# Unread identity products in TensorE's first waits, a first tile normalized in halves, and a later weight decode

## The chip, the cores and the metric

The kernel runs on one core of a Trainium2 chip. The metric is the device time of one execution in microseconds (us); lower is better. TensorE (PE) multiplies, VectorE (DVE) and ScalarE (ACT) work elementwise, GpSimd (POOL) does small things beside them, and SyncE (SP) issues most DMAs. Each engine takes its instructions in the order in which they stand in its queue.

## The reference

Three layers follow each other, for 8 batches of 576 rows and a model width of 512 (8 heads of 64). Cut to what matters:

```
kv  = einsum('bhsd,bhse->bhde', k, v)
out = einsum('bhsd,bhde->bhse', q, kv)
x   = out / sqrt(mean(out*out, -1) + 1e-6) * g_norm       # attention, a norm per head

theta  = x @ w_theta                                      # first mixing layer
zr, zi = x * cos(theta), x * sin(theta)
y = einsum('ts,bsd->btd', w_tok_r, zr) + einsum('ts,bsd->btd', w_tok_i, zi)
u = x + y;  x = u + relu(u @ w_ch)

h = relu(x.T @ w_tok1) @ w_tok2                           # second mixing layer
u = x + h.T;  out = u + relu(u @ w_ch1) @ w_ch2
```

## The kernel before

The weights arrive as 64-bit floats. ACT and DVE decode them into float32: `decode` is one ACT operation and three DVE operations a tile. Nearly every product is then made of three float16 products of high and low parts (`mm3`, L105 to L107). Batch 0 alone is different at its start: its first products run in float32, since nothing is split yet.

That start is what the change touches. A list of words in the main body (L1027) says in which order units of work are recorded for batch 0, and a scheduler orders each engine's queue from that record. The units are generators; every `yield` puts the rest of a unit one step later in the record, and `tc.keep_in_program_order` pins an instruction to its place in it. The units are, in the order of the data:

- `theta_weight(j)`: loads and decodes tile j (of 4) of `w_theta` into `wt` (tiles `wt0r` to `wt3r` hold the raw words).
- `kv`: 40 products of 64x64 from `k` and `v` into one PSUM bank `kvp`, in five groups of 8, one for each pair of loads; ACT and DVE copy the result into `kvbd`.
- `attend(o, r)` (a0 to a4; tile 4 holds the last 64 rows): four products `po`; a square on ACT (L471), a sum on DVE (`ss`, L473), an addition and a power on POOL (`ri`, L474 and L475), the multiplication that makes `x` on DVE (L478), and for batch 0 four transposes on PE (`px`, L488) that ACT copies into `xt` (L490).
- `rotate(o, r)` (r0 to r4): `pt` = xt times `wt` (L563, and L604 for tile 4), then sine and cosine on ACT (`cs`), products with `x` (L586), and the split into `zh` and `zl`.
- `mix_weights`: five tiles `wm0v`, `wm1v`, `wm8v`, `wm2v`, `wm3v` of the token weights, decoded (L164 on ACT; L172, L173, L174 on DVE) and split into `wmh` (ACT, L245) and `wml` (DVE, L247), in between the units above.
- `outer(o, r)` (X0 to X4): the mixing products `pa` and `pb`, float16, which need `zh`, `zl`, `wmh`, `wml`.

DMA engines load all of this in the first 43 us in the order in which SP issues it.

Of the kernel before, what the change touches and what calls it, by code (L numbers as in the profile page):

```python
# [10 lines left out]
F16 = mybir.dt.float16  # L11
F32 = mybir.dt.float32
I32 = mybir.dt.int32
AF = mybir.ActivationFunctionType
ALU = mybir.AluOpType
AX = mybir.AxisListType
# [3 lines left out]
P = 128  # L20
# [8 lines left out]
def attn_mixer_kernel(  # L29
# [4 lines left out]
    nc = tc.nc  # L34
    B, S, DM = k.shape
    D = g_norm.shape[0]
    H = DM // D
# [26 lines left out]
    def bank(name):  # L64
        return ps.tile([P, 512], F32, tag="ps", name=name)
# [48 lines left out]
    nc.gpsimd.memset(rows, 0.0)  # L114
    nc.scalar.dma_start(rows[:1].rearrange("p (i d) -> p i d", d=D), g_norm.unsqueeze(0).unsqueeze(1).to_broadcast([1, P // D, D]))
    pg = bank("pg")
    nc.tensor.transpose(pg[:, :P], rows, ident)
    nc.vector.tensor_copy(gn, pg[:, :1])
    gt, gs = (const.tile([P, 1], F32, name=name) for name in ("gt", "gs"))
# [38 lines left out]
            mybir.DependencyInfo(mybir.DependencyClass.NoSync, mybir.DependencyReason.DATA), reason="behind",  # L158
        )

    def decode(val, raw, behind=None):

        bits = val.bitcast(I32)
        first = nc.scalar.activation(val, raw[..., 1].bitcast(F32), AF.Copy, scale=2.0**-112)  # L164
        if behind is not None:
            gated(first, behind)
        if wp:

            tc.keep_in_program_order(first)
        yield  # L170
        place = placed if wp else lambda ins: ins
        place(nc.vector.tensor_scalar(bits, bits, 3, None, ALU.logical_shift_left))  # L172
        place(nc.vector.scalar_tensor_tensor(bits, raw[..., 0], 29, bits, ALU.logical_shift_right, ALU.bitwise_or))  # L173
        place(nc.vector.scalar_tensor_tensor(bits, raw[..., 1], -(2**31), bits, ALU.bitwise_and, ALU.bitwise_or))  # L174
# [23 lines left out]
    def theta_weight(j):  # L198

        if w_theta.dtype == F32:  # L200
            load(wt[:, j], w_theta[j * P:(j + 1) * P])
            yield
        else:
            raw = stg.tile([P, S, 2], I32, tag="raw", name=f"wt{j}r")[:, :DM]
            load(raw.rearrange("p n w -> p (n w)"), w_theta.bitcast(I32)[j * P:(j + 1) * P])
            yield
            yield from decode(wt[:, j], raw)

    def theta_split(j):

# [214 lines left out]
    def held(o, ins):  # L425
        if o.b == 0:
            tc.keep_in_program_order(ins)

    def kv(o, part):

        if part == 0:
            o.kp = bank(f"kvp{o.b}")[:, :HP * D].rearrange("p (h e) -> p h e", h=HP)
        for r in KV[part]:
            kt, vt = o.kv[2 * r:2 * r + 2]
            for hp in range(HP):
                for i in range(2):
                    cs = slice((2 * hp + i) * D, (2 * hp + i + 1) * D)
                    nc.tensor.matmul(
                        o.kp[i * D:(i + 1) * D, hp, :], kt[:, cs], vt[:, cs],
                        start=r == 0 and hp == 0, stop=r == NR and hp == HP - 1,  # L440
                    )
        if part:
            nc.scalar.activation(kvbd[:D, :, :D], o.kp[:D], AF.Copy)
            nc.vector.tensor_copy(kvbd[D:, :, D:], o.kp[D:])
        yield
        for r in KV[part]:
            if len(o.kv) < 2 * (NR + 1):
                load_kv(o, r + 3)

    def attend(o, r):  # L450
# [17 lines left out]
        x3 = x.rearrange("p (h d) -> p h d", d=D)  # L468
        place = beside(o)
        yield  # L470
        place(nc.scalar.activation(x3, po3, AF.Square, scale=D**-0.5))  # L471
        yield
        held(o, place(nc.vector.tensor_reduce(ss, x3, axis=AX.X, op=ALU.add)))  # L473
        nc.gpsimd.tensor_tensor(ss, ss, eps, ALU.add)  # L474
        nc.gpsimd.tensor_tensor(ri, ss, mhalf, ALU.pow)  # L475
        yield
        yield
        held(o, place(nc.vector.tensor_tensor(x3, po3, ri.unsqueeze(2).to_broadcast([P, H, D]), ALU.mult)))  # L478
        n = SR if r == NR else P
        R, by = o.R[:, :, r * P:r * P + n], SW if r == NR else gs  # L480
        if r == NR and b == 2:
# [52 lines left out]
    def prepare(o):  # L534
        if o.zh is None:

            o.zh = zp.tile([P, KM + 1, DM], F16, tag="zh", name=f"zh{o.b}")
            o.zl = zp.tile([P, KM - 1, DM], F16, tag="zl", name=f"zl{o.b}")
# [446 lines left out]
    def go(unit, lead=False):  # L985
        advance()
        next(unit)
        (leading if lead else pending).append(unit)
# [10 lines left out]
    def flush():  # L999
        while pending or leading:  # L1000
            advance()
# [17 lines left out]
            load_q(o, P)  # L1019
    for part in range(2):  # L1020
        go(kv(o, part))
    prepare(o)
    nc.gpsimd.memset(o.zh[:, 0, :1], 0.0)
    extra += mix_weights()
    nxt = load_heads(1)
    later = channel_weights()
    for what in "a0 . . a1 a4 a2 a3 r0 w r1 r4 w r2 r3 X0 X1 k w w w X4 A0 X2 A1 s0 s1 s2 s3 X3 A4 A2 A3 U".split():  # L1027
        if what == ".":
            advance()
        elif what == "w":  # L1030
            spare()
        elif what == "k":
            for part in range(2):
                go(kv(nxt, part))
        elif what == "U":
            go(mixed(o))
        else:
            unit = {"a": attend, "r": rotate, "X": outer, "s": residual}[what[0].replace("A", "a")]
            go(unit(nxt if what[0] == "A" else o, int(what[1])))
    flush()  # L1040
    extra += later

# [164 lines left out]
```

## Time and profile before

| | |
|---|---|
| median of 3 runs | 1086.23 us (1085.38 to 1087.14) |
| profiled execution, device time | 1085.04 us |
| its span, first to last instruction | 1083.3 us |
| busy, share of the span: PE | 1065.4 us, 98% |
| DVE | 806.9 us, 74% |
| ACT | 565.0 us, 52% |
| POOL | 188.7 us, 17% |

PE is busy nearly all the time, so a change of the time is a change of when PE gets its work at the start, or of what it waits for later. The timeline of one engine shows each instruction's start, its duration, and in brackets how long the engine sat idle before it and what ended that. The chain of waits and the list of PE's waits give the same from PE's side.

### The profile page before, as it was taken

Reading aid. Unit: us, or ns where it says so; the run is one execution under the profiler, and the core shown is the slowest. Engines: PE = TensorE matmul, PEld = TensorE weight load, DVE = VectorE, ACT = ScalarE, POOL = GpSimd, SP = SyncE. Lnnn points to the kernel's source line nnn. Section 1 sums busy time; section 2 is a strip of 40 time slices with the busy share of each in tenths; the row PEclk is TensorE's granted clock in tenths of the full one; section 3 lists DMA queues with packets and bytes.
Section 4 is the critical chain, followed back from the end, with each engine's and each line's share of the span. In section 5 each row is a group of like instructions: output and inputs, shape, how many; then the busy total and the mean of one; then the engine's idle time right before and its main releaser. Section 6 shows DMA issues by size and latency. Waiting matters only on the chain.

```text
span 1083.3 us, 21466 instructions
## 1 busy us (share of the span) xinstructions
PE 1065.4 (98%) x8857; PEld 813.4 (75%) x8857; DVE 806.9 (74%) x1431; ACT 565.0 (52%) x950; POOL 188.7 (17%) x256
## 2 busy tenths in 40 slices
PE   6999999999999999999999999999999999999998
PEld 5677776777668777686777777777777777777776
DVE  4999888788968888788463866858585775858484
ACT  3868456375554655647241736454463645446360
POOL 3140042624517335252000000000000000000000
PEclk9999999999999999999999999999999999999999
DMA  9618369748669387543738111020201101020101
GB/s 361 244 30 243 77 153 264 194 120 221 172 160 242 98 234 188 134 143 74 222 109 288 54 39 51 16 73 12 78 1 46 44 28 61 12 77 8 38 2 44
DMA packets 141366, 126.05 MB, mean 116 GB/s; under 512 B 88212, under 2 KB 117524, under 8 KB 141268
## 3 DMA queue, kind: packets, MB, share of 16 engines
q1 hardware_dynamic: 135888, 104.23, 34.7%
q0 software_dynamic: 5376, 20.45, 5.3%
q8 instruction: 69, 1.13, 0.4%
q14 instruction: 29, 0.24, 0.1%
q10 hardware_dynamic: 4, 0.00, 0.0%
HBM read 74.25 MB, written 29.88 MB: 96 GB/s over the span
## 4 chain that ended last, share of the span: by engine, by line
PE 77%; DVE 9%; DMA 5%; ACT 5%; POOL 2%; issue 1%; SPq 0%; DVEq 0%; POOLq 0%; ACTq 0%
PE pa L105 5%; PE pa L107 5%; PE pa L106 5%; PE na L105 4%; PE na L107 4%; PE na L106 4%; PE py L105 3%; PE py L107 3%; PE py L106 3%; DMA xt<-xs 3%; PE pr L105 2%; PE pr L107 2%; PE pr L106 2%; PE pc L107 2%; PE pc L106 2%; PE pc L105 2%
## 5 line engine op out<-in xcount | busy, mean ns | idle before, releaser
L105 PE MATMUL py<-wmh,zh 128*128 128x320 f16 (+1 forms) x468 | 134.2, 287 | 0.2 <-DMA zh<-zt 0.2
L106 PE MATMUL py<-wml,zh 128*128 128x320 f16 (+1 forms) x468 | 134.2, 287 | 0.0
L107 PE MATMUL py<-wmh,zl 128*128 128x320 f16 (+1 forms) x416 | 119.3, 287 | 0.0
L107 PE MATMUL na<-gh,wbl 128*128 128x288 f16 x384 | 109.3, 286 | 0.0
L106 PE MATMUL pa<-o,wah 128*128 128x288 f16 x384 | 109.2, 286 | 0.0
L106 PE MATMUL na<-gl,wbh 128*128 128x288 f16 x384 | 109.1, 286 | 0.0
L105 PE MATMUL pa<-o,wah 128*128 128x288 f16 x384 | 108.4, 286 | 0.0
L107 PE MATMUL pa<-o,wal 128*128 128x288 f16 x384 | 107.8, 286 | 0.0
L105 PE MATMUL na<-gh,wbh 128*128 128x288 f16 x384 | 106.0, 286 | 0.2
L870 DVE TENSOR_TENSOR gl<-sum,gh 128x1152 f16<-128x1152 f32 x48 | 65.0, 1354 | 21.9 <-ACT gh L869 21.9
L106 PEld LDWEIGHTS <-wbh 128*128 128x128 f16 x672 | 65.7, 98 | 17.8 <-issue 1.0
L106 PEld LDWEIGHTS <-wah 128*128 128x128 f16 x672 | 65.8, 98 | 16.6
L105 PEld LDWEIGHTS <-wah 128*128 128x128 f16 x672 | 65.8, 98 | 16.6
L105 PEld LDWEIGHTS <-wbh 128*128 128x128 f16 x672 | 65.7, 98 | 16.6
L107 PEld LDWEIGHTS <-wal 128*128 128x128 f16 x672 | 65.7, 98 | 16.6
L107 PEld LDWEIGHTS <-wbl 128*128 128x128 f16 x672 | 65.7, 98 | 16.6
L106 PE MATMUL pr<-ul,wch 128*128 128x256 f16 (+1 forms) x256 | 73.0, 286 | 0.0
L105 PE MATMUL pr<-uh,wch 128*128 128x256 f16 (+1 forms) x256 | 72.9, 286 | 0.0
L107 PE MATMUL pr<-uh,wcl 128*128 128x256 f16 (+1 forms) x256 | 72.8, 286 | 0.0
L475 POOL TENSOR_TENSOR ri<-ss,mhalf 128x8 f32<-128x8 f32 x40 | 69.8, 1744 | 2.5
L105 PEld LDWEIGHTS <-zh 128*128 128x128 f16 x576 | 56.4, 98 | 17.0 <-ACT zh L590 1.1
L869 ACT ACTIVATE gh<-sum 128x1152 f16<-128x1152 f32 x48 | 55.6, 1158 | 25.6 <-DVE sum L917 25.6
(304 smaller groups left out, 2922.0 us busy)
## 6 DMA issues: line engine op xcount, KB each, us to landing
c<-u2d SPq DMA_DIRECT2D x32, 288.0 KB, 4.5
out<-c SPq DMA_DIRECT2D x64, 144.0 KB, 1.7
q<-in_q SPq DMA_DIRECT2D x6, 1280.0 KB, 6.9
k<-in_k SPq DMA_DIRECT2D x26, 256.0 KB, 5.6
v<-in_v SPq DMA_DIRECT2D x26, 256.0 KB, 5.5
wa_r<-in_w_ch SPq DMA_DIRECT2D x24, 256.0 KB, 4.3
wb_r<-in_w_ch SPq DMA_DIRECT2D x24, 256.0 KB, 3.8
wad<-wa POOLq DMA_DIRECT2D x24, 224.0 KB, 3.7
```

The costliest lines, as they stand in the source:

```text
L105: nc.tensor.matmul(acc, ah, bh, start=first and i == 0, stop=False, **more)
L106: nc.tensor.matmul(acc, ah, bl, start=False, stop=False, **more)
L107: nc.tensor.matmul(acc, al, bh, start=False, stop=last and i == n - 1, **more)
L475: nc.gpsimd.tensor_tensor(ri, ss, mhalf, ALU.pow)
L869: nc.scalar.activation(h.hi[:, 3:], h.s, AF.Copy)
L870: nc.vector.tensor_tensor(h.lo[:, 3:], h.s, h.hi[:, 3:], ALU.subtract)
```

## The change

Four edits, all in what batch 0 records first. `keep_going(n)` records n products of a float16 view of the identity matrix, 256 columns each, into a PSUM bank `unread` that nothing reads: 18 ahead of everything, 2 ahead of each `kv` group but the first, 6 behind the last group, 8 behind `po` of tile 0 (40 in all). The `kv` products are pinned to their place in the record. Tile 0 alone is squared, summed, raised to the power and multiplied in two halves of four heads (`heads`). Tiles 2 and 3 of `w_theta` have their three DVE operations recorded 5 and 6 steps later and pinned. The list of words moves r0 ahead of a2.

```diff
@@ main body @@
+    unread = bank("unread")
+    eye16 = ident.bitcast(F16)
+
+    def keep_going(n):
+
+        for _ in range(n):
+            tc.keep_in_program_order(nc.tensor.matmul(unread[:, :2 * P], eye16[:, :P], eye16, start=True, stop=True))
+
+    keep_going(18)
     nc.tensor.transpose(pg[:, :P], rows, ident)
@@ decode @@
         yield
-        place = placed if wp else lambda ins: ins
+        for _ in range(ticks):
+            yield
+        place = placed if wp else tc.keep_in_program_order if ticks else lambda ins: ins
@@ theta_weight @@
-            yield from decode(wt[:, j], raw)
+            yield from decode(wt[:, j], raw, ticks=6 if j == KD - 1 else 5 if j == 2 else 0)
@@ kv @@
+            if o.b == 0 and r:
+                keep_going(2)
...
-                    nc.tensor.matmul(
+                    held(o, nc.tensor.matmul(
@@ attend @@
+        heads = [slice(0, H)] if b or r not in (0,) else [slice(0, H // 2), slice(H // 2, H)]
+        for h in heads:
+            place(nc.scalar.activation(x3[:, h], po3[:, h], AF.Square, scale=D**-0.5))
+        yield
+        for h in heads:
+            held(o, place(nc.vector.tensor_reduce(ss[:, h], x3[:, h], axis=AX.X, op=ALU.add)))
+            nc.gpsimd.tensor_tensor(ss[:, h], ss[:, h], eps[:, h], ALU.add)
+            nc.gpsimd.tensor_tensor(ri[:, h], ss[:, h], mhalf[:, h], ALU.pow)
+        yield
+        yield
+        for h in heads:
+            n = h.stop - h.start
+            held(o, place(nc.vector.tensor_tensor(x3[:, h], po3[:, h], ri[:, h].unsqueeze(2).to_broadcast([P, n, D]), ALU.mult)))
@@ main body @@
         go(kv(o, part))
+    keep_going(6)
...
-    for what in "a0 . . a1 a4 a2 a3 r0 w r1 r4 w r2 r3 X0 ...
+    for what in "a0 . . a1 . a4 r0 a2 . a3 w r1 r4 w r2 r3 X0 ...
...
+            if what == "a0":
+                keep_going(8)
```

The scheduler makes more of this than the diff shows. SP's order is the same as before; PE, DVE, ACT and POOL differ until about the first `py` products. Three places matter.

First DVE, from the copy into `kvbd` to the sum of tile 1. `wt2r` and `wt3r` are the raw tiles of the decode, `x00` is tile 0 of batch 0. Before:

```order
L444 COPY kvbd_100<-kvp0_164 64x4x64
L172 TENSOR_SCALAR wt_102<-wt_102 128x512
L173 SCALAR_TENSOR_TENSOR wt_102<-wt2r_151,wt_102 128x512
L174 SCALAR_TENSOR_TENSOR wt_102<-wt2r_151,wt_102 128x512
L473 TENSOR_REDUCE ss00_255<-x00_257 128x8
L172 TENSOR_SCALAR wt_102<-wt_102 128x512
L173 SCALAR_TENSOR_TENSOR wt_102<-wt3r_158,wt_102 128x512
L478 TENSOR_TENSOR x00_257<-po00_250,ri00_256 128x512
L473 TENSOR_REDUCE ss01_268<-x01_270 128x8
L174 SCALAR_TENSOR_TENSOR wt_102<-wt3r_158,wt_102 128x512
```

The same place on DVE in the changed kernel:

```order
L457 COPY kvbd_119<-kvp0_180 64x4x64
L489 TENSOR_REDUCE ss00_282<-x00_284 128x4 x2
L183 TENSOR_SCALAR wt_121<-wt_121 128x512
L184 SCALAR_TENSOR_TENSOR wt_121<-wt2r_170,wt_121 128x512
L185 SCALAR_TENSOR_TENSOR wt_121<-wt2r_170,wt_121 128x512
L496 TENSOR_TENSOR x00_284<-po00_277,ri00_283 128x256 x2
L183 TENSOR_SCALAR wt_121<-wt_121 128x512
L184 SCALAR_TENSOR_TENSOR wt_121<-wt3r_177,wt_121 128x512
L185 SCALAR_TENSOR_TENSOR wt_121<-wt3r_177,wt_121 128x512
L489 TENSOR_REDUCE ss01_310<-x01_312 128x8
```

The sums of tile 0 moved ahead of the decode of `w_theta` tile 2, and its multiplications ahead of the whole decode of tile 3.

Second DVE again, from the multiplication that makes tile 1 (`x01`) to the one that makes tile 2 (`x02`). Before:

```order
L478 TENSOR_TENSOR x01_270<-po01_263,ri01_269 128x512
L473 TENSOR_REDUCE ss02_297<-x02_299 128x8
L173 SCALAR_TENSOR_TENSOR wm0v_344<-wmr0_213,wm0v_344 128x1152
L478 TENSOR_TENSOR x04_281<-po04_274,ri04_280 128x512
L473 TENSOR_REDUCE ss03_311<-x03_313 128x8
L172 TENSOR_SCALAR wm1v_409<-wm1v_409 128x1152
L174 SCALAR_TENSOR_TENSOR wm0v_344<-wmr0_213,wm0v_344 128x1152
L478 TENSOR_TENSOR x02_299<-po02_292,ri02_298 128x512
```

In the changed kernel, one row earlier at the start, since the second decode step of `wm0v` now stands ahead of tile 1:

```order
L184 SCALAR_TENSOR_TENSOR wm0v_397<-wmr0_240,wm0v_397 128x1152
L496 TENSOR_TENSOR x01_312<-po01_305,ri01_311 128x512
L489 TENSOR_REDUCE ss04_333<-x04_335 128x8
L596 SCALAR_TENSOR_TENSOR cs00_348<-cs00_348,pt00_339 128x512
L185 SCALAR_TENSOR_TENSOR wm0v_397<-wmr0_240,wm0v_397 128x1152
L183 TENSOR_SCALAR wm1v_455<-wm1v_455 128x1152
L496 TENSOR_TENSOR x04_335<-po04_328,ri04_334 128x512
L489 TENSOR_REDUCE ss02_354<-x02_356 128x8
L184 SCALAR_TENSOR_TENSOR wm1v_455<-wmr1_242,wm1v_455 128x1152
L258 SCALAR_TENSOR_TENSOR wml_123<-wm0v_397,wmh_122 128x2x576
L604 TENSOR_TENSOR cs00_348<-cs00_348,x00_284 128x1024
L185 SCALAR_TENSOR_TENSOR wm1v_455<-wmr1_242,wm1v_455 128x1152
```

The row that follows is `x02`. Three decode or split steps, a step of the rotation (`cs00`) and a sum stand between tile 4 and tile 2, where two decode steps and a sum stood before.

Third PE, from tile 1's `po` to the transposes of tile 3. Before:

```order
L458 MATMUL po01_263<-kvbd_100,q0_145 128x128 x4
L458 MATMUL po04_274<-kvbd_100,q0_145 128x128 x4
L488 MATMUL px0_283<-ident_78,x00_257 128x128 x4
L458 MATMUL po02_292<-kvbd_100,q0_145 128x128 x4
L458 MATMUL po03_306<-kvbd_100,q0_145 128x128 x4
L563 MATMUL pt00_320<-wt_102,xt00_258 128x512 x2
L488 MATMUL px1_323<-ident_78,x01_270 128x128 x4
L563 MATMUL pt00_320<-wt_102,xt00_258 128x512 x2
L488 MATMUL px4_336<-ident_78,x04_281 128x128 x4
L563 MATMUL pt01_346<-wt_102,xt01_271 128x512 x4
L488 MATMUL px2_354<-ident_78,x02_299 128x128 x4
L604 MATMUL pt04_369<-xt04_282,wt_102 128x64 x16
```

In the changed kernel:

```order
L471 MATMUL po01_305<-kvbd_119,q0_164 128x128 x4
L506 MATMUL px0_320<-ident_78,x00_284 128x128 x4
L471 MATMUL po04_328<-kvbd_119,q0_164 128x128 x4
L581 MATMUL pt00_339<-wt_121,xt00_285 128x512 x4
L471 MATMUL po02_349<-kvbd_119,q0_164 128x128 x4
L506 MATMUL px1_358<-ident_78,x01_312 128x128 x4
L471 MATMUL po03_374<-kvbd_119,q0_164 128x128 x4
L506 MATMUL px4_383<-ident_78,x04_335 128x128 x4
L581 MATMUL pt01_399<-wt_121,xt01_313 128x512 x4
L506 MATMUL px2_406<-ident_78,x02_356 128x128 x4
L622 MATMUL pt04_417<-xt04_336,wt_121 128x64 x16
L506 MATMUL px3_443<-ident_78,x03_381 128x128 x4
```

All of `pt00` now stands ahead of the transposes of tile 1, and three of the five `po` units stand behind the transposes of tile 0, where two did; the order of the transposes (0, 1, 4, 2, 3) is the same.

## Rows read from the trace of the kernel before

**Rows 1.** The page's first part, PE alone: busy time, share, instructions.

```profile
PE 1065.4 (98%) x8857; PEld 813.4 (75%) x8857; DVE 806.9 (74%) x1431; ACT 565.0 (52%) x950; POOL 188.7 (17%) x256
```

**Rows 2.** PE's waits, whole run: total us, times, longest.

```profile
PE pa L107 <- DVE zh L647: 1.2, 1, 1.2
PE pa L105 <- ACT zh L590: 1.0, 1, 1.0
```

**Rows 3.** PE's timeline: start, duration, instruction, count, [idle before, releaser].

```profile
14.36 2.07 PE L458 MATMUL po<-kvbd,q 128*128 128x128 f32 x8 [0.99 <-DVE kvbd L444]
17.36 3.78 PE L458 MATMUL po<-kvbd,q 128*128 128x128 f32 x16 [0.93 <-DMA q<-in_q]
21.25 0.91 PE L488 MATMUL px<-ident,x 128*128 128x128 f32 x4
22.00 1.95 PE L458 MATMUL po<-kvbd,q 128*128 128x128 f32 x16
23.78 1.88 PE L563 MATMUL pt<-wt,xt 128*128 128x512 f32 x4
25.54 0.66 PE L488 MATMUL px<-ident,x 128*128 128x128 f32 x4
...
28.00 0.66 PE L488 MATMUL px<-ident,x 128*128 128x128 f32 x4
...
31.93 0.60 PE L488 MATMUL px<-ident,x 128*128 128x128 f32 x4
...
43.20 0.27 PE L105 MATMUL pa<-wmh,zh 128*128 128x256 f16 x1
43.31 0.27 PE L106 MATMUL pa<-wml,zh 128*128 128x256 f16 x1
...
57.02 0.28 PE L107 MATMUL pa<-wmh,zh 128*128 128x256 f16 x1 [1.15 <-DVE zh L647]
...
71.42 0.30 PE L105 MATMUL py<-wmh,zh 128*128 128x320 f16 x1
...
86.50 0.28 PE L105 MATMUL pa<-wmh,zh 128*128 128x256 f16 x1 [1.00 <-ACT zh L590]
```

**Rows 4.** Busy time in a stretch: PE, PEld, DVE, ACT, POOL, granted clock, DMA share, GB/s.

```profile
12.00:21.80 9.80, 7.76 (x53) 6.99 (x50) 5.25 (x10) 3.50 (x6) 1.88 (x2) 1.00 1.03 402
```

**Rows 5.** DVE's timeline, 15 to 31 us.

```profile
15.35 0.43 DVE L172 TENSOR_SCALAR wt<-wt 128x512 int32<-128x512 int32 x1 [1.05 <-ACT wt L164]
...
17.14 0.68 DVE L473 TENSOR_REDUCE ss<-x 128x8 f32<-128x512 f32 x1
...
20.50 0.69 DVE L478 TENSOR_TENSOR x<-po,ri 128x512 f32<-128x512 f32 x1
...
24.12 0.76 DVE L172 TENSOR_SCALAR wm0v<-wm0v 128x1152 int32<-128x1152 int32 x1 [1.14 <-ACT wm0v L164]
...
29.12 1.35 DVE L174 SCALAR_TENSOR_TENSOR wm0v<-wmr,wm0v 128x1152 int32<-128x1152 int32 x1
30.39 0.69 DVE L478 TENSOR_TENSOR x<-po,ri 128x512 f32<-128x512 f32 x1
```

**Rows 6.** ACT's timeline: the decode of wt2 and of the first mixing weights.

```profile
14.65 0.66 ACT L164 ACTIVATE wt<-wt2r 128x512 f32<-128x512 f32 x1 [0.81 <-DMA wt2r<-in_w_theta]
...
22.84 1.25 ACT L164 ACTIVATE wm0v<-wmr 128x1152 f32<-128x1152 f32 x1
```

**Rows 7.** SP's waits, 0 to 40 us: its k and v loads behind `wmr`.

```profile
SPq L392 <- DMA wmr<-in_w_mix: 6.0, 2, 3.5
```

**Rows 8.** SP's timeline: the load that the longer of those waits held.

```profile
22.53 0.33 SPq L392 DMA_DIRECT2D k<-in_k  x1
```

**Rows 9.** POOL's timeline: the addition with DVE idle, the power, an addition beside L174.

```profile
17.98 0.20 POOL L474 TENSOR_TENSOR ss<-ss,eps 128x8 f32<-128x8 f32 x1 [10.96 <-DVE ss L473]
18.26 1.68 POOL L475 TENSOR_TENSOR ri<-ss,mhalf 128x8 f32<-128x8 f32 x1
...
29.09 1.45 POOL L474 TENSOR_TENSOR ss<-ss,eps 128x8 f32<-128x8 f32 x1
```

More of the change, by code (lines that the diff above doesn't have):

```diff
@@ L159, in gated, with decode @@
         )
-    def decode(val, raw, behind=None):
+    def decode(val, raw, behind=None, ticks=0):
         bits = val.bitcast(I32)
@@ L437, in kv @@
                     cs = slice((2 * hp + i) * D, (2 * hp + i + 1) * D)
-                    nc.tensor.matmul(
+                    held(o, nc.tensor.matmul(
                         o.kp[i * D:(i + 1) * D, hp, :], kt[:, cs], vt[:, cs],
                         start=r == 0 and hp == 0, stop=r == NR and hp == HP - 1,
-                    )
+                    ))
         if part:
@@ L470, in attend @@
         yield
-        place(nc.scalar.activation(x3, po3, AF.Square, scale=D**-0.5))
+        heads = [slice(0, H)] if b or r not in (0,) else [slice(0, H // 2), slice(H // 2, H)]
+        for h in heads:
+            place(nc.scalar.activation(x3[:, h], po3[:, h], AF.Square, scale=D**-0.5))
         yield
-        held(o, place(nc.vector.tensor_reduce(ss, x3, axis=AX.X, op=ALU.add)))
-        nc.gpsimd.tensor_tensor(ss, ss, eps, ALU.add)
-        nc.gpsimd.tensor_tensor(ri, ss, mhalf, ALU.pow)
+        for h in heads:
+            held(o, place(nc.vector.tensor_reduce(ss[:, h], x3[:, h], axis=AX.X, op=ALU.add)))
+            nc.gpsimd.tensor_tensor(ss[:, h], ss[:, h], eps[:, h], ALU.add)
+            nc.gpsimd.tensor_tensor(ri[:, h], ss[:, h], mhalf[:, h], ALU.pow)
         yield
         yield
-        held(o, place(nc.vector.tensor_tensor(x3, po3, ri.unsqueeze(2).to_broadcast([P, H, D]), ALU.mult)))
+        for h in heads:
+            n = h.stop - h.start
+            held(o, place(nc.vector.tensor_tensor(x3[:, h], po3[:, h], ri[:, h].unsqueeze(2).to_broadcast([P, n, D]), ALU.mult)))
         n = SR if r == NR else P
@@ L1026, in attn_mixer_kernel @@
     later = channel_weights()
-    for what in "a0 . . a1 a4 a2 a3 r0 w r1 r4 w r2 r3 X0 X1 k w w w X4 A0 X2 A1 s0 s1 s2 s3 X3 A4 A2 A3 U".split():
+    for what in "a0 . . a1 . a4 r0 a2 . a3 w r1 r4 w r2 r3 X0 X1 k w w w X4 A0 X2 A1 s0 s1 s2 s3 X3 A4 A2 A3 U".split():
         if what == ".":
```

## The prediction

> **What bounds the kernel now.** I read the busy shares first: PE is busy 98% of the span [rows 1]. So only what PE waits for can be won, or lost. The list of PE's waits comes next. Behind the start there are two of about 1 us, one for the low half of the last rows (at 57.02 us) and one for `zh` of batch 1 (86.50 us) [rows 2, 3]. The rest lies ahead of 21.25 us, so I laid the timelines of the engines side by side. PE runs without a gap worth naming from the first transposes at 21.25 us to the first mixing product at 43.20 us, and on to the wait ahead of 57.02 [rows 3]. Ahead of that it waits for `kvbd` (0.99), for a load of `q` (0.93), and runs slowly: 16 rows of `po` take 3.78 us at 17.36 and 1.95 us at 22.00 [rows 3], 236 against 122 ns. That is TensorE's lower level, 1.2 GHz, against 2.4 GHz, though the granted clock prints 1.00 for that stretch [rows 4]. The chain of waits shows why px0 is no earlier: the load of `w_theta` tile 3, its decode on ACT and DVE, and only behind these the multiplication of tile 0 at 20.50 [rows 5]. From there the chain runs through DVE and ACT, not PE, to 86.5 us. DVE is the second bound: it hardly idles from 24.12 on.
>
> **The change, step by step.** All times are of the profiled execution: span 1083.3 us, device time 1085.04, so 1.74 lie around the span; its time is 1.19 below the median of 1086.23. For each engine I took the changed order and laid the durations of before end to end, each instruction behind its own inputs; on DVE the next one starts some 0.08 ahead of an end, as 29.12 + 1.35 and 30.39 show [rows 5], so a sum of 0.68 counts 0.6.
>
> *Products.* One costs 0.11 us, the step from 43.20 to 43.31 [rows 3], or 0.22 at the lower level. The 18 stand where PE has nothing to do before the first loads. The 2 ahead of a group and the 6 behind the last lie in waits for loads and for `kvbd`. The 8 behind tile 0's `po` (0.9 to 1.8 us) lie between its end, about 15.3 us, and the `q` load that ends PE's wait at 17.36 [rows 3]. If they raise the level by then, `po` of tile 1 takes 0.9 instead of 1.9 us. They cost nothing there, and no load: SP's later loads of `k` wait for `kvp` groups to free tiles, but the one at 22.53 was held by another load [rows 7, 8]. If the level is still low, everything shifts: about 1.0 us for `po` of tile 1 and its successors.
>
> *Tile 0.* ACT decodes tile 2 of `w_theta` from 14.65 to 15.31 [rows 6] and then squares in two halves, to about 16.0. DVE sums two halves (half of 0.68 each [rows 5], 16.4), decodes tile 2 (17.14 - 15.35 = 1.79 [rows 5], to 18.2) and multiplies. POOL now has two additions and two powers where it had one of each. An eight-column power took 1.68 us, an addition 0.20 with DVE idle, but 1.45 at 29.09, when it ended just behind the decode step that DVE ran from 29.12 to 30.47 [rows 5, 9]. No row shows a four-column power: between 0.82 (half) and 1.68 (no saving). I take 0.95, near half, as the addition's 0.20 says that little of the 1.68 is a fixed part. The second addition meets the decode of tile 2 and ends with it, 18.3; the second power at 19.4. px0 starts at 18.6 and ends at 20.0. With 1.68, the second half comes at 20.9.
>
> The Trainium skill (GPSIMD Engine Reference, Specifications) says that POOL shares SBUF interfaces with VectorE and contends with its instructions in a two-port mode or with two SBUF inputs. That speaks against halves beside a decode; the rows agree. By rows without that contention the second power would end 0.6 earlier and px0 with it; the sum would stay, since DVE then waits longer for the load named below.
>
> *Rotation 0.* `pt00` starts at 20.6 instead of 23.78 [rows 3]. **Here the change is 3.2 us ahead.**
>
> *Where it is lost.* On DVE the first decode step of `wm0v` waits for ACT, and ACT for the load `wmr`. A later load of SP waited 3.5 us for that one to land, and left at 22.53 [rows 7, 8]; SP's order is the same, so ACT, done with tile 0 and 4 by 21.8, starts at 22.5 instead of 22.84 [rows 6], and DVE's step at 23.9 instead of 24.12 [rows 5]. The decode of `w_theta` tile 3 and the sum of tile 1, which now stand between, are done by 22.2, and the last quarter of `pt00` needs that decode only at 23.2: they are hidden. Of 3.2 us, 0.2 are left on DVE. Tile 1 used to be multiplied behind that step; now the second step (1.35 [rows 5]) stands ahead of it too: 23.9 + 0.8 + 1.3 + 0.7 = 26.7. So px1 is at 26.75 instead of 25.54 [rows 3], and PE, done with `pt00` and `po` of tile 2 at 24.9, **waits 1.85 us**. Between tile 1 and tile 4 stand a sum (0.6), a step of the rotation (0.6), the third decode step (1.3) and the first of `wm1v` (0.7): tile 4 is ready at 30.45, px4 at 30.5 instead of 28.00. PE did 0.5 of px1 and 0.9 of `po`, and **waits 2.4 us**. `pt01` stands behind px4: 31.0 to 34.4. Between tile 4 and tile 2 stand a sum (0.6), a decode step (1.3), the split of `wm0v` (1.3), the product with `x` (1.1, from the 1.35 of a row 1152 wide), another decode step (1.3). The split also waits for ACT; I allow 0.3, between 0 and the 1.14 that DVE waited for ACT at 24.12 [rows 5]. Tile 2 starts at 36.2 instead of 30.39 and px2 at 36.9 instead of 31.93: **PE waits 2.5 us.** From px2 to the first `pa` PE has 43.20 - 31.93 = 11.3 us of work [rows 3]; it follows almost without a gap, as tile 3 comes in time, and `pa` starts at 48.2 instead of 43.20: **5.0 us late.**
>
> *What comes back.* DVE has fewer steps left from there to the low half of the last rows, as three of them moved ahead: it is ready at 61.0, when PE, 5.0 late, asks for it. So the wait of 1.15 at 57.02 [rows 2, 3] goes, and with it some 0.3 of stalls behind it. The wait at 86.50 stays: DVE and ACT come to it about as late as PE. **Sum: +5.0 - 1.5 = +3.5 us.** Behind 90 us the orders agree again and PE is the bound, so nothing returns.
>
> Laid the same way, the order of before gives 43.2 us for the first `pa`, as its trace has it, and 72.1 for the first `py`, 0.7 more than its trace [rows 3]; so I trust the sum to about 1 us. With a four-column power of 1.68 it is +4.4.
>
> **The rivals.** *The level rises late.* In before the level had not risen when `po` ran at 17.36, behind groups of `kvp` and a first `po`; it had at 22.00 [rows 3]. The 18 products are 4.0 us of work at the lower level, and PE waits for loads behind them. If it rises only between 14 and 21 us, `po` of tile 0 ends 1 to 1.8 us later, the 8 products reach past 17.36, and the sum is +4.6 to +6.5; 1091.7 us. Chance 0.23.
>
> *The level falls again.* The three new waits of 1.85 to 2.5 us are longer than any in before behind 21.25 us, and none there lowered the level. If, of the 11.3 us of work behind px2, the first 2 run at the lower level, 2 us are lost where PE is the bound: +5.5, 1091.7 us. Chance 0.07. The Trainium skill (TensorE: Matmul & The Clock Gate, HAM oscillation) says that waits between bursts of products can put the clock back to half; no wait of before shows it.
>
> *It comes back in the mixing.* If tile 2 is multiplied by about 35 us (ACT's split free at once, and the POOL addition not held), and both waits [rows 2] go in full, 5.0 - 1.2 - 1.5 - 1.0 = +1.3: 1087.5 us, within 0.2%. Against it: `zh` at 86.50 hangs on DVE, which is late too. Chance 0.13.
>
> *Faster.* PE keeps its lead of rotation 0. If px1, px4 and px2 find their tiles in time, `pa` starts at 18.6 + 21.95 + 0.9 = 41.5, 1.7 early: 1084.5 us. It decides at tile 1: DVE would have to multiply it by 25 us, and there the queue holds two decode steps that wait for a load of 22.5 us. Chance 0.07.
>
> **How the numbers follow.** Forecast, chance 0.50: 1086.23 + 3.5 = 1089.7 us. 0.2% (2.2 us) is about what a measurement of this kernel can tell from no change. The forecast and the first two rivals are slower by more: 0.80. Within it: 0.13. Faster: 0.07. The range leaves out the faster case, the lower half of the third rival (0.06) and the top of the first two (0.06): 1087.4 to 1092.5.
>
> **What would show it.** Right: px1 near 26.8, px4 near 30.5, px2 near 37 us, each behind a wait of about 2 us for DVE, `pa` near 48, no wait at the low half, one of about 1 us at 90. `po` of tile 1 in 0.9 us shows that the products raised the level. Wrong: px1 by 25.5, or px2 by 33 us; or a first mixing product that waits longer than PE is late.

## The result, and the profile after

| | before | after |
|---|---|---|
| device time, median of 9 runs each (lowest to highest) | 1086.16 us (1084.94 to 1087.96) | 1093.49 us (1088.40 to 1095.36) |
| ratio, 95% interval | | 1.0059 [1.0044, 1.0074] |
| profiled execution, device time (span) | 1085.04 us (1083.3) | 1095.36 us (1093.6) |

The change makes the kernel slower, by 7.3 us between the medians; the forecast was 3.5 us, and the time lies above the end of the range, 1092.5 us. The nine runs are not spread evenly. Each has a mean granted clock: two with 0.998 took 1088.40 and 1088.91 us, one with 0.996 took 1089.45, six with 0.995 or 0.994 took 1092.04 to 1095.36. So there are two losses to look for, one that every execution has and one that comes with the clock.

PE's waits in the profile after (total us, times, longest). The first row is new, three waits for DVE's `x`; of the two of before in [rows 2] the one for the low half of `zh` is gone and the one for ACT's `zh` has grown from 1.0 to 1.6 us.

```profile
PE px L506 <- DVE x L496: 5.8, 3, 2.8
...
PE pa L105 <- ACT zh L608: 1.6, 1, 1.6
```

PE's timeline of after, which answers to [rows 3] (start, duration, instruction, count, [idle before, releaser]):

```profile
15.09 1.16 PE L471 MATMUL po<-kvbd,q 128*128 128x128 f32 x8 [0.24 <-DVE kvbd L457]
18.54 1.16 PE L471 MATMUL po<-kvbd,q 128*128 128x128 f32 x8 [1.42 <-DMA q<-in_q]
19.75 0.44 PE L506 MATMUL px<-ident,x 128*128 128x128 f32 x2
20.90 0.44 PE L506 MATMUL px<-ident,x 128*128 128x128 f32 x2 [0.71 <-DVE x L496]
...
22.18 3.70 PE L581 MATMUL pt<-wt,xt 128*128 128x512 f32 x8
...
26.86 0.66 PE L506 MATMUL px<-ident,x 128*128 128x128 f32 x4
...
30.76 0.66 PE L506 MATMUL px<-ident,x 128*128 128x128 f32 x4 [2.34 <-DVE x L496]
...
37.60 1.11 PE L506 MATMUL px<-ident,x 128*128 128x128 f32 x4 [2.75 <-DVE x L496]
38.51 6.92 PE L622 MATMUL pt<-xt,wt 128*128 128x64 f32 x32
45.23 1.06 PE L506 MATMUL px<-ident,x 128*128 128x128 f32 x4
...
53.54 0.27 PE L105 MATMUL pa<-wmh,zh 128*128 128x256 f16 x1
```

px1, px4 and px2 stand within 0.7 us of the forecast, though no wait stands before px1. Behind px2 the forecast no longer holds: `pt` of tile 4 takes 6.92 us for the same 32 rows that took 3.68 us in before, and `pa` starts at 53.54 us, 10.3 late where 5.0 were forecast. The row of before:

```profile
32.37 3.68 PE L604 MATMUL pt<-xt,wt 128*128 128x64 f32 x32
```

The stretches of the trace of after say why (from:to, length, busy PE, PEld, DVE, ACT, POOL, granted clock, DMA share, GB/s):

```profile
9.78:13.20 3.42, 3.37 (x39) 2.24 (x38) 0.00 (x0) 0.00 (x0) 0.00 (x0) 0.51 1.09 373
13.20:37.09 23.89, 16.79 (x100) 10.71 (x98) 18.45 (x26) 15.14 (x23) 10.10 (x10) 1.00 1.02 397
37.09:47.33 10.24, 9.73 (x42) 9.15 (x43) 6.21 (x8) 5.27 (x9) 1.84 (x2) 0.50 0.55 218
```

The clock fell to its lower level, 1.2 GHz, at 37.09 us, inside the wait of 2.75 us before px2, and stayed there for 10.24 us in which PE was the bound. In the low stretch at 9.78 us PE works on the `kvp` groups and the products between them, and it costs little: from the first `kvp` product to `po` of tile 0 pass 7.28 us (7.81 to 15.09), in before 7.05 (7.31 to 14.36). A mean clock of 0.998 stands for one such short stretch, which in ten of the sixteen profiles with the products is this one (in those of `fillpx14` and `less_dot`, also at 0.998, it lies later); 0.994 or 0.995 stands for 10 to 14 us of low level in all, in one piece or in several.

Now DVE's timeline of after, 22 to 37.5 us; `ss` is a tile's sum, `x` its multiplication. The sums and multiplications of tiles 1, 4 and 2 come in the order sum, multiplication, sum, multiplication:

```profile
22.71 0.68 DVE L489 TENSOR_REDUCE ss<-x 128x8 f32<-128x512 f32 x1
24.05 0.76 DVE L183 TENSOR_SCALAR wm0v<-wm0v 128x1152 int32<-128x1152 int32 x1 [0.66 <-ACT wm0v L173]
24.84 1.36 DVE L184 SCALAR_TENSOR_TENSOR wm0v<-wmr,wm0v 128x1152 int32<-128x1152 int32 x1
26.12 0.68 DVE L496 TENSOR_TENSOR x<-po,ri 128x512 f32<-128x512 f32 x1
26.72 0.68 DVE L489 TENSOR_REDUCE ss<-x 128x8 f32<-128x512 f32 x1
...
30.01 0.69 DVE L496 TENSOR_TENSOR x<-po,ri 128x512 f32<-128x512 f32 x1
30.62 0.68 DVE L489 TENSOR_REDUCE ss<-x 128x8 f32<-128x512 f32 x1
31.21 1.35 DVE L184 SCALAR_TENSOR_TENSOR wm1v<-wmr,wm1v 128x1152 int32<-128x1152 int32 x1
33.18 1.36 DVE L258 SCALAR_TENSOR_TENSOR wml<-wm0v,wmh 128x1152 f16<-128x1152 f32 x1 [0.63 <-ACT wmh L256]
34.46 1.22 DVE L604 TENSOR_TENSOR cs<-cs,x 128x1024 f32<-128x1024 f32 x1
35.59 1.35 DVE L185 SCALAR_TENSOR_TENSOR wm1v<-wmr,wm1v 128x1152 int32<-128x1152 int32 x1
36.86 0.68 DVE L496 TENSOR_TENSOR x<-po,ri 128x512 f32<-128x512 f32 x1
```

In before two sums stood ahead of the first of these multiplications, and then each sum one tile ahead (the next multiplication, of tile 2, is the last row of [rows 5]):

```profile
21.11 0.68 DVE L473 TENSOR_REDUCE ss<-x 128x8 f32<-128x512 f32 x1
...
22.30 0.68 DVE L473 TENSOR_REDUCE ss<-x 128x8 f32<-128x512 f32 x1
...
24.80 0.68 DVE L478 TENSOR_TENSOR x<-po,ri 128x512 f32<-128x512 f32 x1
25.40 0.68 DVE L473 TENSOR_REDUCE ss<-x 128x8 f32<-128x512 f32 x1
...
27.26 0.69 DVE L478 TENSOR_TENSOR x<-po,ri 128x512 f32<-128x512 f32 x1
```

That shows on POOL, which makes the addition and the power between a sum and its multiplication. Its waits for DVE from 20 to 42 us, before and then after:

```profile
POOL ss L474 <- DVE ss L473: 1.9, 1, 1.9
```

```profile
POOL ss L490 <- DVE ss L489: 10.5, 4, 3.9
```

In before POOL worked through one tile after the other; in after it stands idle between any two, as the next sum waits behind the last multiplication. The prediction had worked these times out, but had named another cause for them, the decode steps of `wm0v` and `wm1v`.

### The profile page after: what moved, and what is told of

Same layout as the page of the kernel before. It is cut to its first block, busy times and chain, and to the rows that moved or that the text cites. A ratio compares the mean times of both kernels' runs of the same rounds, so it can differ in the third digit from the quotient of the medians.

```text
span 1093.6 us, 21549 instructions
## 1 busy us (share of the span) xinstructions
PE 1073.3 (98%) x8897; PEld 818.6 (75%) x8897; DVE 808.7 (74%) x1433; ACT 565.6 (52%) x951; POOL 186.2 (17%) x258
## 3 DMA queue, kind: packets, MB, share of 16 engines
q8 instruction: 70, 1.15, 0.4%
## 4 chain that ended last, share of the span: by engine, by line
PE 85%; DVE 6%; DMA 3%; ACT 3%; POOL 2%; issue 1%; SPq 0%; POOLq 0%; DVEq 0%; ACTq 0%
PE pa L105 5%; PE pa L106 5%; PE pa L107 5%; PE na L105 4%; PE na L107 4%; PE py L106 4%; PE py L107 4%; PE na L106 4%; PE py L105 4%; PE pr L105 3%; PE pr L107 3%; PE pr L106 3%; PE po L471 2%; PE pc L107 2%; PE pc L106 2%; PE pc L105 2%
## 5 line engine op out<-in xcount | busy, mean ns | idle before, releaser
L491 POOL TENSOR_TENSOR ri<-ss,mhalf 128x8 f32<-128x8 f32 (+1 forms) x41 | 68.9, 1680 | 2.5
```

The lines of the kernel that those rows point to most:

```text
L491: nc.gpsimd.tensor_tensor(ri[:, h], ss[:, h], mhalf[:, h], ALU.pow)
```

## Experiments: does the clock cost the second half?

All times are medians; the kernel before ran beside every group, at 1085.46 to 1086.24 us. The kernel `fill` puts more unread products into PE's waits and changes nothing else:

```diff
@@ attend, ahead of the transposes px @@
+            keep_going({1: 12, 4: 18, 2: 20}.get(r, 0))
             for kk in range(KD):
```

**fill.** 

> The changed kernel with 50 more unread identity products: 12 ahead of the transposes px1, 18 ahead of px4, 20 ahead of px2, so that they run in the three waits for the DVE's x that the trace of after shows (1.85 to 2.75 us each); nothing of the computation moves. Theory (order plus clock: the new order costs 3.5 us, and the waits let the TensorE clock fall from 37.1 to 47.3 us in many executions, which costs the other 4): 1089.7 (1088.5 to 1090.5) with a narrow spread, granted clock 1.00 from 30 to 50 us, pt04 back from 6.9 to about 3.7 us, pa at 48.2 to 49. Rival A (the whole 7 us is the order on the DVE, the clock a bystander): 1093.5, pa at 53 or later though the clock is high. Rival B (the identity products themselves cost, by what they draw or delay): 50 more make it worse than 1093.5.

Measured: 1090.75 us (1088.98 to 1100.44, 10 runs), ratio 1.0053 [1.0033, 1.0073], 0.25 us above the range expected and not with a narrow spread. (Of the three waits that the text above gives to the trace of after the first is only forecast: the trace has 2.34 and 2.75 us, and 0.71 for the second half of tile 0.) Eight runs have a mean clock of 0.997 or 0.998 and a median of 1090.28 us; the two others took 1093.35 and 1100.44. In after seven of nine were below 0.997. The ratio's interval overlaps that of after, so the total alone does not settle it; the clock of each run and the trace do. PE's timeline and the stretch in which after ran low:

```profile
30.97 0.60 PE L507 MATMUL px<-ident,x 128*128 128x128 f32 x4
...
37.45 0.66 PE L507 MATMUL px<-ident,x 128*128 128x128 f32 x4 [0.26 <-DVE x L496]
37.94 3.68 PE L623 MATMUL pt<-xt,wt 128*128 128x64 f32 x32
...
49.00 0.27 PE L105 MATMUL pa<-wmh,zh 128*128 128x256 f16 x1
```

```profile
37.09:47.33 10.24, 9.96 (x54) 6.86 (x54) 9.29 (x14) 8.35 (x15) 1.84 (x2) 1.00 0.55 217
```

px2 starts within 0.15 us of after's, so the order's loss is the same; at the full clock `pt` of tile 4 takes 3.68 us and `pa` starts 4.5 us sooner. Rivals A and B are out as they were put: at a high clock `pa` is at 49.00 and not at 53 or later, and 50 more products do not make it worse than 1093.5. A smaller price of the products in the waits is not excluded: the eight runs at a high clock stand 3.2 to 5.8 us above the before beside them, after's two at 0.998 only 2.2 and 2.8 above theirs. Why the clock fell in two of the ten runs all the same, in one to a mean of 0.989, no trace here shows. The profiled execution took 1088.98 us, 3.94 more than the profiled one of before.

**fillpx2** keeps only the 20 products, `{2: 20}`. 

> The changed kernel with 20 unread identity products ahead of the transposes px2 alone; the waits before px1 and px4 stay empty. Which of the three waits lets the clock fall: in the profile of after the fall is at 37.1 us, inside the wait before px2. Theory (that wait does it): like the kernel with all three filled, 1090 (1089 to 1091.5) with the mean clock at 0.997 or 0.998 in most executions. Rival (any of the three can): half or more of the executions fall still, at 27 to 33 us, and the median is 1092 or more.

**fillpx14** keeps only the others, `{1: 12, 4: 18}`. 

> The changed kernel with 12 unread identity products ahead of px1 and 18 ahead of px4; the wait before px2, the longest, stays empty. Theory (the wait before px2 lets the clock fall): like after, 1092 to 1095 in most executions with a mean clock of 0.995 or less, the profile low from some 37 us on, pt04 near 6.9 us. Rival (any of the three can, or all together do): about half of the executions keep the clock, median 1090 to 1092.

Measured: fillpx2 1091.85 us (1088.52 to 1093.68, 6 runs), five of six at 0.997 or more; fillpx14 1092.62 us (1091.27 to 1096.40, 6 runs), five of six below. By the clocks the wait before px2 matters most. The times do not separate the two kernels (ratios 1.0053 [1.0038, 1.0069] and 1.0068 [1.0051, 1.0085]), the forecast of fillpx2's median was missed by 0.35 us, and the profiles show why the rival, that any of the three waits can do it, has a point. In fillpx2 the clock fell behind the empty wait of 2.34 us before px4, and once more far behind:

```profile
32.90:36.40 3.50, 3.50 (x6) 1.36 (x5) 3.40 (x4) 1.77 (x3) 3.40 (x2) 0.52 1.00 348
...
186.70:190.00 3.30, 3.01 (x8) 1.10 (x9) 0.52 (x2) 0.29 (x1) 0.00 (x0) 0.52 0.96 282
```

The profiled run of fillpx14 is the one of its six at 0.998. In it the empty wait before px2 did not lower the clock, where `pt` of tile 4 near 6.9 us was expected:

```profile
38.27 0.66 PE L507 MATMUL px<-ident,x 128*128 128x128 f32 x4 [2.45 <-DVE x L496]
38.76 3.68 PE L623 MATMUL pt<-xt,wt 128*128 128x64 f32 x32
```

## Experiments: which edit costs the order's share?

Four switches make the kernels of this section out of the changed kernel (`keeponly` uses the last three together, and so on by the table):

```diff
@@ no products: every keep_going call goes @@
-    keep_going(18)
@@ no halves @@
-        heads = [slice(0, H)] if b or r not in (0,) else [slice(0, H // 2), slice(H // 2, H)]
+        heads = [slice(0, H)]
@@ no ticks @@
-            yield from decode(wt[:, j], raw, ticks=6 if j == KD - 1 else 5 if j == 2 else 0)
+            yield from decode(wt[:, j], raw, ticks=0)
@@ old list @@
-    for what in "a0 . . a1 . a4 r0 a2 . a3 w r1 ...
+    for what in "a0 . . a1 a4 a2 a3 r0 w r1 ...
```

| kernel | products | halves | ticks | new list | median us (runs) | ratio, 95% interval | runs at 0.997 or more |
|---|---|---|---|---|---|---|---|
| keeponly | x | | | | 1084.93 (11) | 0.9994 [0.9985, 1.0002] | 10 |
| keephalf | x | x | | | 1085.58 (10) | 1.0000 [0.9990, 1.0009] | 9 |
| keeptick | x | | x | | 1089.38 (6) | 1.0038 [1.0023, 1.0052] | 4 |
| oldlist | x | x | x | | 1091.39 (5) | 1.0051 [1.0039, 1.0063] | 0 |
| nohalf | x | | x | x | 1094.27 (5) | 1.0084 [1.0052, 1.0116] | 1 |
| notick | x | x | | x | 1097.65 (4) | 1.0105 [1.0088, 1.0122] | 0 |
| nokeep | | x | x | x | 1091.40 (6) | 1.0054 [1.0036, 1.0073] | 6 |
| after | x | x | x | x | 1093.49 (9) | 1.0059 [1.0044, 1.0074] | 2 |

**keeponly.** 

> Of the change only the identity products and the kvp products held in program order: no halves, no ticks, the word list of before. Theory: the clock is up by about 13 us instead of 21.8, the first tile's products shorten by about 1 us, no new wait; x's order on the DVE is that of before, pa 1 to 1.5 us earlier, of which the mixing gives back most (the waits behind 57 us): 1085 to 1086.3, granted clock 1.00 from 13 to 60 us. Rival B (products cost): 1087.5 or more. Rival A (order): 1086 and nothing gained before pa.

**keephalf.** 

> Identity products, kvp held in order, and the halves; the word list of before, no ticks. Theory: no new wait, pa 1.5 us earlier than before, most of it given back behind 57 us: 1084.5 to 1086, like the products alone (1084.9). Rival C (the halves cost): 1087 to 1089, x0's second half late and POOL's later additions held.

**keeptick.** 

> Identity products, kvp held in order, and the ticks on the third and last w_theta tile; no halves, the word list of before. What the earlier runs left open is which of the three edits (halves, ticks, list) costs the 3.5 us of order. Theory (the list and the ticks together put the wm0 decode ahead of x1, x4 and x2): ticks alone give one wait of 2 us before px1, which eats what the products gained (px1 25.5, pa 43.2 as before): 1086 (1085.5 to 1087) where the clock holds, some 3 more where it falls behind that wait. Rival C (the halves cost, by holding POOL and the x's behind it): 1085, as with the products alone (1084.9).

**oldlist** (it has 40 products, not the 50 of this text). 

> The changed kernel with the word list of before (a0 . . a1 a4 a2 a3 r0 w ...); products, halves and the ticks on the third and last w_theta tile stay. Theory: r0's early start (pt00 at 21 to 22 us instead of 23.8) and with it the two waits before px4 and px2 go; one wait before px1 of about 3.4 us stays, since the ticks still put the wm0 decode ahead of x1. px2 some 1.5 to 2 us late, pa 2 late: 1088 to 1088.5 where the clock holds, and up to 3 more where it falls behind the one long wait. Rival A (order alone, clock a bystander, 7 us): 1088 to 1091 with no difference between executions. Rival B (products cost): near 1093, since all 50 are still there.

**nohalf.** 

> The changed kernel without the halves. Theory: the three waits (before px1, px4, px2) are those of after, pa 5 us late: 1089 to 1090 where the clock holds, 1092 to 1095 where it falls, so a median near that of after. Rival C (the halves cost): 1085 to 1087, no wait over 1 us before px4 and px2.

**notick.** 

> The changed kernel without the ticks: products, halves and the new word list stay. Theory: the new list alone makes the waits, now as one of some 5.6 us before px2, since w_theta's decode goes ahead of x1 and the wm0 decode ahead of x2; pa 5.5 late and two more waits behind 57 us: 1093 to 1095 where the clock holds, 1096 and more where it falls behind the long wait. Rival D (the ticks make the loss, the list does not): 1085 to 1087.

**nokeep.** 

> The changed kernel without the identity products: halves, ticks and the new word list stay. Theory: the same three DVE waits as in after (before px1, px4, px2) and the clock low until some 22 us as in before: pa 5.5 to 6 us late, 1089.5 to 1091; whether the clock falls again behind the waits is the open point (it does: 1093 and more; it does not: 1090.5). Rival B (products cost): back to 1086 to 1087.5. Rival A (order alone): 1093.

By keeponly and keephalf products and halves cost nothing that shows (rivals B and C are out). Ticks and list cost, each by itself: with the ticks alone 3.6 us (1.9 to 4.2 in the runs that kept the clock, where I had expected 0.2; in its profile PE waits 1.57 us for tile 0 and 1.50 for tile 1), with the list but no ticks 11.9 us, with a fall in every run (in its profile one wait of 5.25 us before px2, where 5.6 was expected), which ends rival D. In these totals, falls included, the ticks make the new list cheaper, not dearer. Without products (`nokeep`) 5.6 us are lost, so the products don't make the loss. The last column cannot be compared for this kernel: its profile, at 1.000, records no low stretch at the start, so 0.997 stands here for falls elsewhere, some 6 us of low level (an estimate from the span and the two levels). Its two runs at 1.000 lost 4.01 and 4.55 us, and three of the other four 6.7 to 9.2; the fourth, 1088.11 us at 0.997, does not fit, and that stays open. In its profile PE waits before px4 (2.27), px2 (1.28) and px3 (1.04), and `pa` is 6.8 us late, where 5.5 to 6 were expected.

`oldlist` shows the second loss behind a single wait. Its px1, and the stretch around it:

```profile
28.08 1.12 PE L506 MATMUL px<-ident,x 128*128 128x128 f32 x4 [2.89 <-DVE x L496]
```

```profile
27.00:34.20 7.20, 6.12 (x14) 3.44 (x15) 7.12 (x10) 3.13 (x4) 6.38 (x5) 0.53 1.04 390
```

All five runs of it had 0.995 or less. I had expected 1088 to 1088.5 where the clock holds, and up to 3 more where it falls; it held in none, and the median of 1091.39 us is the second case.

## Experiments: what holds x1, x4 and x2 on DVE?

**nodec_after** leaves out the six DVE decode steps that the prediction blamed; **nodec_before** is the same in the kernel before.

```diff
@@ decode @@
         yield
         for _ in range(ticks):
             yield
+        if bare:
+            return
@@ mix_weight: the call of decode gets bare=j in (0, 1) @@
```

> The changed kernel without the DVE's three decode steps of wm0 and of wm1 (that part of w_mix is left undecoded; all else stays). The prediction put the waits before px1, px4 and px2 down to these decode steps standing ahead of x1, x4 and x2. Decode theory: without them px1 is at 25.6, px4 by 28.5 and px2 by 33 us, no wait over 0.8 us behind px1, pa at 42 to 44, 1085 to 1087. Rival F (each tile's sum now stands behind the tile before's multiplication on the DVE, so that the chain of sum, POOL's addition and power, and multiplication is laid bare for every tile, decode or not): px4 at 29.8 behind a wait of 2.8, px2 at 36.0 behind 2.3, pa 47.3, 1088 to 1090 where the clock holds and 3 or more above where it falls.

> The same six decode steps left out of the kernel before, as the control. Both theories: PE was the bound there from 21 us on, so pa stays near 43.4 (42.7 to 44) and the time at 1085.5 to 1088; only the difference of the changed kernel to this one is read.

Measured: 1092.55 us (1091.05 to 1098.38, 8 runs) against 1086.52 us of the control (nine of its ten runs; one of 2273.14 us is left out), ratios to before 1.0066 [1.0046, 1.0086] and 1.0003 [0.9991, 1.0016]. The decode theory is out: PE's px4 and px2 wait nearly as in after, in a trace whose clock is 1.00 there,

```profile
30.13 0.66 PE L508 MATMUL px<-ident,x 128*128 128x128 f32 x4 [2.36 <-DVE x L498]
...
36.33 0.66 PE L508 MATMUL px<-ident,x 128*128 128x128 f32 x4 [2.10 <-DVE x L498]
```

while DVE now stands idle and waits, first for POOL's power and then for ACT's sines:

```profile
29.38 0.69 DVE L498 TENSOR_TENSOR x<-po,ri 128x512 f32<-128x512 f32 x1 [1.21 <-POOL ri L493]
...
34.45 1.23 DVE L606 TENSOR_TENSOR cs<-cs,x 128x1024 f32<-128x1024 f32 x1 [2.51 <-ACT cs L603]
35.59 0.68 DVE L498 TENSOR_TENSOR x<-po,ri 128x512 f32<-128x512 f32 x1
```

Rival F holds for tile 4, in time and place. For tile 2 the row names another: rotation 0's product `cs` stands ahead of x2, and it waits for ACT. px4 and px2 come 0.6 and 1.3 us sooner than in after, where the decode theory wanted 2.3 and 4.6. `pa` is at 47.65 us, near F's 47.3. The total (1091.05 to 1094.59 us in the six runs at 0.997 or more) is 1 us and more above what F gave for a high clock, since behind `pa` nothing came back: in the profile PE still waits 1.1 us at the low half, and 2.3 us for ACT's `zh`. Against its control's profile (`pa` at 44.25 us, device time 1087.72) `pa` is 3.4 us late and the time 3.3 longer.

**nopow_after** leaves out POOL's powers of tiles 1, 4, 2 and 3; **nopow_before** does so in before.

```diff
@@ attend, in the loop over heads @@
+            if b == 0 and r:
+                nc.gpsimd.tensor_tensor(ri[:, h], ss[:, h], eps[:, h], ALU.add)
+                continue
```

> The changed kernel without POOL's powers of tiles 1, 4, 2 and 3 of batch 0 (their x is multiplied by the sum itself, so that part is left out); the decode steps all stay. Rival F (the bared chain): px4's wait falls from 2.4 to 0.8 or less and px2's from 2.5 to 1 or less, px2 by 34.5, pa by 46. Decode theory: what stands on the DVE between the tiles is unchanged, so px4 still waits about 1.9 and px2 2.5 to 3.4, px2 at 36 to 36.5, pa at 48 to 49.

> The same four powers left out of the kernel before, as the control. Both theories: pa at 42.7 (42.3 to 43.2), 1085 to 1086.5.

Measured: 1095.08 us (4 runs) against 1086.28 us of the control. PE's two waits:

```profile
29.98 0.66 PE L509 MATMUL px<-ident,x 128*128 128x128 f32 x4 [0.86 <-DVE x L499]
...
37.92 1.11 PE L509 MATMUL px<-ident,x 128*128 128x128 f32 x4 [3.85 <-DVE x L499]
```

A shorter chain frees px4 (2.34 to 0.86), as rival F said, but px2 comes no sooner (37.92 against 37.60 us): three decode steps, the split and the product of rotation 0 stay ahead of x2. PE's wait there is longer because PE is there 0.8 us sooner. The decode theory was nearer for px2's wait (2.5 to 3.4 expected, 3.85 measured) and wrong for px4's (1.9). So two things hold the tiles, not one. The clock fell in all four runs (0.990 to 0.995), which makes the total useless for the order.

**late_r0** tests the second: r0 goes back behind a3, the dots stay.

```diff
-    for what in "a0 . . a1 . a4 r0 a2 . a3 w r1 ...
+    for what in "a0 . . a1 . a4 a2 . a3 r0 w r1 ...
```

> The changed kernel with r0 back behind a3 in its word list; the two new dots, the halves, the ticks and the products stay. Theory G (the wait before px2 is r0's own: its product with x, which waits for ACT's sines, and the split of wm0 stand ahead of x2 on the DVE because r0 comes early): that product now stands behind x2, and px2, which takes the place of pt00, waits 1 us or less and starts at 34 to 34.5 us instead of 37.6; PE's whole wait moves before px1 (4 to 5 us, as no pt00 fills the time), pa 48 to 49, 1089.5 to 1091 where the clock holds, 1093 and more where it falls behind that long wait. Rival F alone (only the bared chain): px2 near 37 behind a wait of 2 us or more as in after.

**less_dot** gives the sum of tile 3 its old place back: `a4 r0 a2 a3` instead of `a4 r0 a2 . a3`. 

> The changed kernel with one dot fewer in its list (a2 a3 instead of a2 . a3), so that tile 3's sum stands ahead of x2 on the DVE again as in before; r0 stays early. Theory F and G together: the waits before px1 and px4 stay (1.1 to 1.9 and 2.4); x2 is no earlier (px2 at 37.5 to 38, still behind r0's product and the split), but x3 comes 1.2 us sooner and PE meets fewer waits behind: pa 47, 1087 to 1088.5 where the clock holds, 3 or more above where it falls. If one tile's chain is worth nothing: as after, 1089 where the clock holds, pa at 48.2 or later.

Measured: late_r0 1095.51 us (1094.25 to 1098.19, 4 runs), less_dot 1091.73 us (1087.72 to 1094.56, 6 runs). PE in late_r0:

```profile
27.31 1.12 PE L506 MATMUL px<-ident,x 128*128 128x128 f32 x4 [4.60 <-DVE x L496]
...
35.00 0.60 PE L506 MATMUL px<-ident,x 128*128 128x128 f32 x4
```

```profile
25.50:32.50 7.00, 5.19 (x16) 3.71 (x17) 6.92 (x9) 3.47 (x4) 4.06 (x4) 0.51 1.04 393
```

Theory G holds: with r0 late, DVE multiplies tile 2 at 33.59 instead of 36.86 us, rotation 0's product follows at 41.43, and px2 comes at 35.00 instead of 37.60 us, without a wait and 0.5 later than expected. But all the waiting is now before px1, 4.60 us, the clock falls there for 7 us, and the sum is worse. In less_dot the four runs at 0.997 or 0.998 took 1087.72, 1088.78, 1090.97 and 1092.49 us, where 1087 to 1088.5 was expected; they are 2.3 to 7.0 us above their before, and after's two at 0.998 are 2.2 and 2.8 above theirs, so a gain from the one tile is not shown. The edit also did more than it was meant to: the scheduler put `pt` of tile 4 ahead of px2 (at 35.14 and 38.66 us in the profile). So px2 does not wait; PE waits 1.68 us before px3 instead, the clock falls there for 3.4 us, and `pa` starts at 49.91.

## Is there a better version?

**keeponly_again** is keeponly once more. 

> The identity products and the held kvp alone, once more, since it stood 0.06% under the kernel before with an interval that included it: 1085 (1084.3 to 1085.6) against 1085.8 if the products' gain is real, at or over 1085.8 if the first comparison was chance.

**keepmore** puts more products behind `po` of tile 0 in keeponly.

```diff
             if what == "a0":
-                keep_going(8)
+                keep_going(22)
```

> The kernel with the products alone, and 22 of them instead of 8 behind the first tile's po, so that PE works through the wait for the second load of q (1.7 us there). Theory (waits of that size let the clock fall now and then, by the 0.996 and 0.997 of some executions): those executions go, median 1084 to 1085. If the q load lands at 17.4 us the products end behind it and po01 is up to 0.6 us late, which the wait before px0 hides. Rival B (products cost): above 1085.8.

Measured: keeponly_again 1085.28 us (12 runs), ratio 0.9992 [0.9983, 1.0002]. The median lies in the range expected for a real gain. Twice the products alone stand 0.9 us under before, twice with an interval that reaches 1; the two intervals together would end just below 1 (an estimate, 0.9999). They are better than the changed kernel, and better than before by so little that it is not safely shown. keepmore brings no gain: 1087.61 us (1083.35 to 1089.45, 12 runs), ratio 1.0006 [0.9993, 1.0019], where 1084 to 1085 was expected. Its profile shows `po` of tile 1 without a wait, as meant, and a fall far behind, in a wait of 2.77 us for a transposing DMA ahead of `ph`:

```profile
179.00:187.00 8.00, 6.12 (x15) 2.14 (x16) 3.42 (x5) 3.10 (x6) 0.00 (x0) 0.57 1.02 257
```

Why that wait was longer than the 1.1 us of before in this execution, and whether the products have to do with it, was not tried further.

## Right and wrong, step by step

- **Products: right.** In `keeponly` they cost nothing that shows, and `po` of tile 0 took 1.16 instead of 2.07 us, that of tile 1 the same. The rival of a level that rises late did not happen: the clock was at 1.00 from 13.2 us.
- **Tile 0: px0 0.9 us too early, with no effect.** The four-column powers took 1.13 and 1.01 us, not 0.95. `fill`, with its `q` load at the forecast time, has px0 at 19.50 instead of 18.6 and `pt00` at 21.93 instead of 20.6. So PE had 1.85 us in hand there, not 3.2, and the wait forecast before px1 was not there to be seen: `po` of tile 2 ended just as x1 came. px1 itself was right (26.75 forecast, 26.86 measured).
- **The waits: right in time, incomplete in cause.** px4 30.5 and 30.76, px2 36.9 and 37.60, `pa` 48.2 and, at a high clock, 49.00. The steps that the prediction laid end to end were the ones that stood there. But it took the decode steps for what held the tiles, and without them px4 and px2 come only 0.6 and 1.3 us sooner: px4 waits for the bared chain of sum, power and multiplication, px2 for rotation 0's product behind ACT's sines. Where several chains end at about the same time, as here, taking the longest away leaves the next.
- **What comes back: right in size.** In the profile of `fill` `pa` is 5.8 us late and the device time 3.9, so 1.9 came back (1.5 forecast): the wait at the low half, and half of the wait for ACT's `zh` (0.5 us instead of 1.0), which the prediction had let stand.
- **"The level falls again": this step failed.** It had a chance of 0.07 and a price of 2 us, for the first 2 of the 11.3 us of work behind px2. By the mean clocks it happened in seven of nine runs. In the profile it lasted 10.24 us and cost 6.92 - 3.68 for `pt` of tile 4, 1.11 - 0.66 for px2, 1.06 - 0.66 for px3, and 0.6 for the `pt` products behind it: 4.7 us, as much as the way from px2 to `pa` grew (15.94 us, 11.27 in before). It fits the difference of the medians, 7.3, less the 2.2 and 2.8 us of after's two runs at 0.998. The argument against it was that no wait in before had lowered the level; but the waits there were 1.15 us at most, and the new ones before px4 and px2 2.3 and 2.8, so before could not say anything about them. The Trainium skill (TensorE: Matmul & The Clock Gate, HAM oscillation), which the prediction cites, describes a kernel with products of about 2 us between waits of 3 to 5 us for loads that put the clock back every time. The traces here agree in kind: the clock fell behind waits of 2.3 to 5.3 us. But it did not fall in every run, and a row below shows a fall behind shorter waits.

The +3.5 us of the order thus stands at 2.2 and 2.8 in after's two runs that kept the clock, at 3.2 to 5.8 (median 4.5) in `fill`'s eight, and at 4.0 and 4.6 in the two of `nokeep` at 1.000. How the 7.3 us divide between order and clock is therefore known only to some 2 us. The range was missed by a rival that was named and priced too low.

## What to carry to other kernels

Before a tile's work is moved ahead in an in-order queue, look at how far the next tile's first step ran ahead of this tile's last one: the chain over three engines was hidden here only while two tiles were in flight. A forecast that ends with new TensorE waits like those here (2.3 to 2.8 us) should carry the price of the clock's fall in its main case, worked out over the whole stretch of TensorE-bound work behind the wait; unread products in the wait are a cheap test of it.

## What was not expected of the hardware

- The fall is not the same in each execution of one kernel: 1088.4 and 1095.4 us for the same program. The low stretches lasted 3.4 to 13.6 us in the profiles of this study. All seven waits for `x` of 2.75 us and more in these profiles were followed by the low level, and of seven between 2.1 and 2.45 us one was; yet a wait of 2.8 us for ACT's `zh` in `keeptick` was not. Nor does it need one long wait: in fillpx14 the clock fell at 20.3 us, where PE had waited 1.20, 0.26 and 0.71 us:

```profile
20.30:23.50 3.20, 3.20 (x12) 2.53 (x11) 2.41 (x4) 1.84 (x4) 0.48 (x2) 0.50 1.02 410
```

- A short one is not rare even in before: 26 of its 92 runs beside the experiments had a mean clock under 1.00 (0.996 to 0.999), at 1084.16 to 1089.35 us.
- A power over four columns took 1.01 to 1.40 us on POOL where one over eight mostly took 1.64: the two halves of after, 1.13 and 1.01, cost nearly a third more than one whole.
